# The end of an FFT-convolution kernel on one core: the last scan slot split by frequency, the last transposes by token, the stores cut smaller, the residual added per channel quarter

## The chip, the cores and the metric

The kernel runs on one core of a Trainium2 chip (trn2). It is one program. The metric is the device time of one execution in microseconds (us), as the median of several runs. The profile is of one execution by itself and has its own time. The engines are called as the profile calls them: PE (matmuls), DVE (vector), ACT (scalar), POOL (GpSimd) and SP, which only issues DMA transfers; "SPq" and "ACTq" are DMA issues on SP's and ACT's queue.

## The reference

The input `u` has 2048 tokens (L) of 512 channels (D). Its layer norm feeds two branches, which are multiplied and added to the input:

```python
x = A_u
xn = _layernorm(x)
s = irfft(rfft(xn, 2L) * rfft(K, 2L))[:L] + xn * Dskip   # K: a 2048-tap filter per channel, from 128 complex modes
h = gelu_tanh(xn @ w1 + b1)                              # 512 -> 1792
g = silu(h @ w2 + b2)                                    # 1792 -> 512
out = x + s * g
```

Everything is float32.

## The kernel before, in words

The long first part (some 400 us) does the layer norm, both matrix products of the second branch and the filters. A written-out list of tokens fixes its order, and the change does not touch it. The second part does the convolution, and the order there is the order of the code: each engine works through its instructions as `slot` and the lines behind the loop issue them.

The convolution is a two-step Fourier transform with length 2048 = 32 x 64. The channels go in four blocks `b` = 0 to 3 of 128 channels, and every block takes eight slots `g` = 0 to 7. A slot handles four of the 32 outer frequencies:

- `second_dft` (L881): PE makes the inner transform of signal and filter for these frequencies, in a tile `s`, in two PSUM banks.
- `spectrum` (L889): ACT copies the signal half to SBUF (`uh`). `product` (L898): DVE multiplies it with the filter half, in two instructions of 512 elements for each partition, to `t`.
- `combine` (L906, L908): DVE makes real and imaginary part `Y` of the complex product; both its inputs lie in SBUF. It is called once for two slots, in the last block's last two slots once each.
- `back_dft` (L919): PE transforms eight frequencies back into two banks `sa`, one for each `a`; `es` chooses which of its four steps `e` run.
- `back_out` (L929): `sa` goes to SBUF (`Z`). `turn` (L935): DVE transposes 32x32 blocks of `Z` to `T`, in halves `i` of 1024 elements. `Z` and `T` are kept for each half `h` of the frequencies.
- `last_dft` (L966): PE ends the transform in banks `y`, adding `h` = 0 and `h` = 1. `last_gate` (L973; L979 for the last block): DVE multiplies `y` with the gate `g` read back from memory. `last_add` (L983): adds `x`, by default on POOL. `store` (L988): four DMA transfers, one for each channel group `c`.

The outputs of block `b` are finished in slots 4 to 7 of block `b + 1`. For block 3 nothing follows, so the lines L1098 to L1114 finish it alone: the second half of the last `back_dft`, the `y` products, copies shared by ACT and DVE, transposes, and then two halves of the tokens (0 to 7, 8 to 15 of 16 for each partition), each gated by DVE, added by DVE (5 tokens) and POOL (3 tokens), and stored by four transfers of 128 KB, two on SP's queue and two on ACT's.

A tile is one object for the bookkeeping of waits: where two engines touch the same PSUM bank, one waits for the other. A transfer signals its landing on one of eight semaphores (`DMAHW0` to `DMAHW7` in the order below), in turn, and a transfer whose semaphore was used before waits, on its queue, for the landing of that earlier transfer.

Of the kernel before, what the change touches and what calls it, by code (L numbers as in the profile page):

```python
# [11 lines left out]
F32 = mybir.dt.float32  # L12
# [8 lines left out]
P = 128  # L21
L, D, NS, F = 2048, 512, 128, 1792
G = D // P
NF = F // P
KD = D // P
N1, N2 = 32, 64
NB = 4
# [5 lines left out]
NQ = L // P  # L33
# [135 lines left out]
def kernel(  # L169
# [126 lines left out]
    SB = {}  # L296
# [499 lines left out]
    side, xf, fp = {}, {}, {}  # L796
# [75 lines left out]
    def second_dft(b, g):  # L872
        mc = SB["mc"]
        p = SB["ps"].tile([P, 2, 2, 2, 2, N2], F32, tag="ri", name=f"s2_{b}_{g}", bufs=2)
        for jj in range(2):
            for o in range(2):
                for c in range(2):
                    for ka in range(2):
                        for r in range(2):
                            k, h = 8 * (g // 2) + 4 * ka + 2 * (g % 2) + jj, slice(r * 64, (r + 1) * 64)  # L880
                            PE.matmul(p[ka * 64:(ka + 1) * 64, r, o, :, jj], mc[h, k, ((0, 2), (1, 0))[c][o], :],  # L881
                                      xf[b][h, c, :, k, :], start=(c == 0), stop=(c == 1), skip_group_check=True)
        sp[b, g] = p
# [10 lines left out]
    def product(b, g):  # L894
        p, uh = sp.pop((b, g))
        for i in range(2):
            t = sm[b, g // 2][i].rearrange("p o r (h a) x -> p h o r (a x)", h=2)[:, g % 2]
            V.tensor_mul(t, p[:, i, :, 1].unsqueeze(1).to_broadcast([P, 2, 2, P]), uh)  # L898

    def combine(b, j, c, eng, js=slice(0, 4)):  # L900
        t, w = sm[b, j]
        if (b, j) not in yy:
            yy[b, j] = SB["pm"].tile([P, 2, 4, P], F32, tag="Y", name=f"Y_{b}_{j}", bufs=2)
        Y = yy[b, j][:, c].rearrange("p j (r x) -> p r j x", r=2)
        if c == 0:
            eng.tensor_sub(Y[:, :, js], t[:, 0, :, js], w[:, 1, :, js])  # L906
        else:
            eng.tensor_add(Y[:, :, js], t[:, 1, :, js], w[:, 0, :, js])  # L908
# [13 lines left out]
    def back_out(b, j, eng=A, m=slice(0, N2)):  # L922
        if (b, "Z", j // 2) not in yy:
            yy[b, "Z", j // 2] = SB["pm"].tile([P, N2, 2, N1 // 2], F32, tag="Z", name=f"Z{b}_{j // 2}", bufs=2)
        for a, p in enumerate(yy[b, j, "p"]):
            k = 8 * (j % 2) + 4 * a
            dst = yy[b, "Z", j // 2][:, m, :, k:k + 4]
            src = p.rearrange("p k (c n) -> p n c k", c=2)[:, m]
            A.copy(dst, src) if eng is A else eng.tensor_copy(dst, src)  # L929

    def turn(b, h, i, n=2):
        if i == 0:
# [34 lines left out]
                              start=(h == 0), stop=(h == 1), skip_group_check=True)  # L967

    def last_gate(b):
        g = gx[b][0].rearrange("p n (a c r) -> p r a n c", a=2, r=2)  # L970
        for q in range(G):
            d = g[:, q // 2, q % 2]
            V.tensor_mul(d, gx[b, "y"][q].rearrange("p (n c) -> p n c", c=N1), d)  # L973

    def last_gate_wide(b, n):
        g = gx[b][0].rearrange("p n (a c r) -> p r a n c", a=2, r=2)
# [1 line left out]
            d = g[:, r, :, n]  # L978
            V.tensor_mul(d, gx[b, "w"][r].rearrange("p a (n c) -> p a n c", c=N1)[:, :, n], d)  # L979

    def last_add(b, n, eng=GP):
        g, x = gx[b]
        eng.tensor_add(x[:, n], g[:, n], x[:, n])  # L983

    def store(b, n=slice(0, NQ), qs=(SY,) * G):
        x = gx[b][1]
# [5 lines left out]
    def slot(b, g):  # L992
# [6 lines left out]
        second_dft(b, g)  # L999
        for x in back:  # L1000
            back_dft(*x)
        if u:
# [2 lines left out]
            last_dft(b - 1)  # L1005
        if last and g == 7:
            back_dft(b, 3, (0, 1))
        spectrum(b, g)
        for x in back:
            back_out(*x)  # L1010
        if u:
            first_out(b + 1, *u, engs, A)
        product(b, g)
        if u:
            first_out(b + 1, *u, engs, V)
        if (b, g) == (0, 0):
            new_gate(0)
        if last and g > 5:
            for c in range(2):
                combine(b, i, c, V, slice(2 * g - 12, 2 * g - 10))  # L1020
        elif g % 2:
# [46 lines left out]
    with tc.manual_schedule():  # L1068
# [43 lines left out]
        last_add(b, slice(8, 13), V)  # L1112
        last_add(b, slice(13, NQ), GP)
        store(b, hi, (SY, A, SY, A))  # L1114
    pz.close()
    p2.close()

# [27 lines left out]
```

## Time and profile before

| what | us |
|---|---|
| median of three runs | 553.2 (553.17 to 555.86) |
| the profiled execution, its time | 554.85 |
| the profiled execution, its span from first to last instruction | 553.1 |
| busy: PE, DVE, ACT, POOL | 526.9, 456.0, 387.0, 289.8 |

The time of an execution is 1.75 us longer than its span (554.85 against 553.1); the rest lies outside the instructions. In the rows, times are from the span's start; "x2" means two instructions merged in one row, and the text in brackets gives the engine's idle time before the row and what ended it. The granted clock was 0.994 over the span.

### The profile page before, as it was taken

Reading aid. Unit: us, or ns where it says so; the run is one execution under the profiler, and the core shown is the slowest. Engines: PE = TensorE matmul, PEld = TensorE weight load, DVE = VectorE, ACT = ScalarE, POOL = GpSimd, SP = SyncE. Lnnn points to the kernel's source line nnn. Section 1 sums busy time; section 2 is a strip of 40 time slices with the busy share of each in tenths; the row PEclk is TensorE's granted clock in tenths of the full one; section 3 lists DMA queues with packets and bytes.
Section 4 is the critical chain, followed back from the end, with each engine's and each line's share of the span. In section 5 each row is a group of like instructions: output and inputs, shape, how many; then the busy total and the mean of one; then the engine's idle time right before and its main releaser. Section 6 shows DMA issues by size and latency. Waiting matters only on the chain.

```text
span 553.1 us, 17527 instructions
## 1 busy us (share of the span) xinstructions
PE 526.9 (95%) x7439; PEld 419.6 (76%) x7439; DVE 456.0 (82%) x684; ACT 387.0 (70%) x566; POOL 289.8 (52%) x385
## 2 busy tenths in 40 slices
PE   8899999999999999999999999999999999999971
PEld 7577777777777777777777777777878997989860
DVE  5899998999998899997987978968247667688784
ACT  3589997986698998768989798997264553534320
POOL 5639586685967669957809846641220203413042
PEclk9999999999999999999999999999999999999997
DMA  8959336266659293446068129403896485536943
GB/s 186 291 161 317 86 96 204 69 190 208 178 173 278 101 290 104 140 113 179 24 194 241 46 72 203 79 20 108 314 372 92 112 153 106 164 81 159 208 99 76
DMA packets 110538, 86.92 MB, mean 157 GB/s; under 512 B 43414, under 2 KB 88730, under 8 KB 110460
## 3 DMA queue, kind: packets, MB, share of 16 engines
q1 hardware_dynamic: 100592, 67.45, 46.3%
q0 software_dynamic: 8768, 17.83, 10.7%
q8 instruction: 58, 0.95, 0.7%
q10 hardware_dynamic: 1100, 0.53, 0.4%
q14 instruction: 20, 0.16, 0.1%
HBM read 52.23 MB, written 33.55 MB: 155 GB/s over the span
## 4 chain that ended last, share of the span: by engine, by line
PE 71%; DVE 19%; issue 5%; POOL 2%; DMA 1%; ACT 1%; POOLq 0%; SPq 0%; DVEq 0%; ACTq 0%
PE s L881 10%; PE z L290 8%; PE z L291 7%; PE z L292 7%; PE f L251 7%; PE f L253 7%; PE f L252 7%; PE s L861 6%; PE kg L651 5%; PE sa L919 4%; PE ph L590 2%; DVE hl L277 2%; DVE e L636 2%; PE y L966 1%; DVE e L640 1%
## 5 line engine op out<-in xcount | busy, mean ns | idle before, releaser
L613 POOL TENSOR_TENSOR mm<-mm,rc 128x32 f32<-128x32 f32 (+4 forms) x150 | 111.4, 742 | 11.8
L290 PE MATMUL z<-w2h,hh 128*128 128x512 f32 x224 | 97.9, 437 | 0.0
L251 PE MATMUL f<-xh,w1h 128*128 128x512 f32 x220 | 91.9, 418 | 0.1
L292 PE MATMUL z<-w2h,hl 128*128 128x512 f32 x224 | 88.6, 395 | 1.0 <-DVE hl L277 1.0
L291 PE MATMUL z<-w2l,hh 128*128 128x512 f32 x224 | 88.6, 396 | 0.0
L253 PE MATMUL f<-xh,w1l 128*128 128x512 f32 x220 | 87.0, 395 | 1.5 <-DVE w1l L236 1.5
L252 PE MATMUL f<-xl,w1h 128*128 128x512 f32 x220 | 86.7, 394 | 0.0
L881 PE MATMUL s<-X,mc 64*64 64x128 f32 x2048 | 64.1, 272 | 2.6 <-issue 2.0
L898 DVE TENSOR_TENSOR t<-s,uh 128x512 f32<-128x512 f32 x64 | 41.0, 682 | 30.3 <-ACT uh L889 30.0
L881 PEld LDWEIGHTS s<-X,mc 64*64 64x64 f32 x2048 | 56.0, 133 | 9.4 <-issue 5.6
L292 PEld LDWEIGHTS z<-w2h,hl 128*128 128x128 f32 x224 | 42.1, 188 | 11.8 <-DVE hl L277 1.8
L610 POOL COPY mm<-rc 128x32 f32<-128x32 f32 x30 | 15.7, 524 | 66.4 <-DVE e L643 50.9
L636 DVE TENSOR_TENSOR e<-mm,ra 128x1024 f32<-128x1024 f32 x32 | 46.7, 1459 | 4.6 <-POOL mm L613 3.0
L253 PEld LDWEIGHTS f<-xh,w1l 128*128 128x128 f32 x220 | 41.3, 188 | 12.0 <-DVE w1l L236 2.2
L277 DVE TENSOR_TENSOR hl<-hf,hh 128x512 fp32r<-128x512 f32 x56 | 47.2, 846 | 3.3 <-ACT hh L271 3.3
L290 PEld LDWEIGHTS z<-w2h,hh 128*128 128x128 f32 x224 | 42.5, 190 | 9.0
L604 DVE SCALAR_TENSOR_TENSOR ra<-ra,ph 128x512 f32<-128x512 f32 x64 | 43.6, 682 | 6.8 <-ACT ra L598 5.9
L251 PEld LDWEIGHTS f<-xh,w1h 128*128 128x128 f32 x220 | 41.5, 189 | 9.7 <-ACT hf L265 0.6
L291 PEld LDWEIGHTS z<-w2l,hh 128*128 128x128 f32 x224 | 42.3, 189 | 7.9
L252 PEld LDWEIGHTS f<-xl,w1h 128*128 128x128 f32 x220 | 41.4, 188 | 9.0
L983 POOL TENSOR_TENSOR xb<-gb,xb 128x512 f32<-128x512 f32 x12 | 17.6, 1497 | 53.8 <-DVE gb L973 30.4
L640 DVE TENSOR_TENSOR e<-mm,ra 128x1024 f32<-128x1024 f32 x32 | 45.4, 1420 | 0.0
(171 smaller groups left out, 1104.5 us busy)
## 6 DMA issues: line engine op xcount, KB each, us to landing
x<-in_A_u_dram SPq DMA_DIRECT2D x16, 256.0 KB
xs<-x SPq DMA_DIRECT2D x16, 256.0 KB
xt_h<-xh POOLq DMA_DIRECT2D x4, 1024.0 KB, 5.3
xt_l<-xl POOLq DMA_DIRECT2D x4, 1024.0 KB, 7.8
kgd<-ko SPq DMA_DIRECT2D x32, 128.0 KB
za<-zo SPq DMA_DIRECT2D x4, 1024.0 KB
xh<-xt_h POOLq DMA_DIRECT2D x4, 1024.0 KB, 6.7
xl<-xt_l POOLq DMA_DIRECT2D x4, 1024.0 KB, 10.0
```

What stands on the lines that cost most here:

```text
L251: PE.matmul(p, wh[:, k, :], xh[:, k, :], start=(k == 0), stop=False)
L252: PE.matmul(p, wh[:, k, :], xl[:, k, :], start=False, stop=False)
L253: PE.matmul(p, wl[:, k, :], xh[:, k, :], start=False, stop=(k == KD - 1))
L277: V.tensor_sub(hl, hf, hh)
L290: PE.matmul(z, hh[:, s], wh, start=(f0 == 0 and not rows), stop=False)
L291: PE.matmul(z, hh[:, s], wl, start=False, stop=False)
L292: PE.matmul(z, hl[:, s], wh, start=False, stop=(f0 == FA - 1))
L604: V.scalar_tensor_tensor(ra[:, 0, c], ra[:, 1, c], MAGIC, p, op0=ALU.subtract, op1=ALU.subtract)
L613: GP.tensor_mul(mv[:, :, 0:3:2, w:2 * w], mv[:, :, 0:3:2, 0:w], rc[:, 2 + 2 * i:4 + 2 * i, :].rearrange("p j c -> p c j").unsqueeze(3).to_ ...
L636: V.tensor_mul(e1, m1.unsqueeze(1).to_broadcast([P, 2, CH, N1]), ra[:, :, :, :N1])
L640: V.tensor_mul(e2[:, :, :, :H], m2[:, :, :H].unsqueeze(1).to_broadcast([P, 2, CH, H]), ra[:, :, :, dn])
L881: PE.matmul(p[ka * 64:(ka + 1) * 64, r, o, :, jj], mc[h, k, ((0, 2), (1, 0))[c][o], :], xf[b][h, c, :, k, :], start=(c == 0), stop=(c == 1 ...
```

## The change

- In slot 7 of the last block, `last_second`, `last_product` replace `second_dft`, `spectrum`, `product`: the tile's layout puts the pair of frequencies `jj` outside, and copy, products and `combine` run for each `jj` by itself.
- `last_out` replaces `back_out` for the second half of the last block's frequencies. `Z` is laid out by token half `i` first, and ACT does all the copies, of the steps 0 and 1 of the last `back_dft` before the steps 2 and 3. `last_turn` transposes one token half, and `last_half` makes `y` for that half from all frequencies, with 256 columns instead of 512.
- The second transposition of the first frequency half moves from slot 5 to the end of slot 7.
- The last gates, adds and stores go over the tokens 0-3, 4-7, 8-11, 12-13, 14-15. DVE does all the adds; there are 20 transfers instead of 8.
- For the blocks 0 to 2, POOL adds `x` for each channel quarter `q` right behind that quarter's gate (rows of 32 elements, every second one in memory), and no longer by groups of four tokens. The stores stand where they stood.

```diff
+    def last_second(b, g):
...
+        p = SB["ps"].tile([P, 2, 2, 2, 2, N2], F32, tag="ri", name=f"s2_{b}_{g}", bufs=2)
+        for jj in range(2):
...
+                            PE.matmul(p[ka * 64:(ka + 1) * 64, r, jj, o], mc[h, k, ((0, 2), (1, 0))[c][o], :],
+                                      xf[b][h, c, :, k, :], start=(c == 0), stop=(c == 1), skip_group_check=True)
+    def last_product(b, g, jj):
+        p, uh = sp[b, g]
+        q = p[:, :, jj].rearrange("p r o u x -> p o r u x")
+        A.copy(uh[:, jj], q[:, :, :, 0])
+        for i in range(2):
+            V.tensor_mul(sm[b, g // 2][i][:, :, :, 2 * (g % 2) + jj],
+                         q[:, i, :, 1].unsqueeze(1).to_broadcast([P, 2, 2, N2]), uh[:, jj])
+        for c in range(2):
+            combine(b, g // 2, c, V, slice(2 * (g % 2) + jj, 2 * (g % 2) + jj + 1))
+    def last_out(b, j, k0, k1):
...
+        for i in range(2):
+            for a, p in enumerate(yy[b, j, "p"]):
+                k = 8 * (j % 2) + 4 * a
+                A.copy(yy[b, "Z", 1][:, i, :, :, :, k + k0:k + k1],
+                       p[:, k0:k1].rearrange("p k (c g i m) -> p i g m c k", c=2, g=4, i=2)[:, i])
+    def last_turn(b, i):
...
+        V.transpose(yy[b, "T", 1][:, i].rearrange("p g m c -> p (g m c)"),
+                    yy[b, "Z", 1][:, i].rearrange("p g m c k -> p (g m c k)"))
+    def last_half(b, i):
+        for g in range(G):
+            for q in range(G):
+                r = slice(q * N1, (q + 1) * N1)
+                PE.matmul(gx[b, "y"][q][g * N1:(g + 1) * N1, i * 256:(i + 1) * 256], SB["gc"][r, 1],
+                          yy[b, "T", 1][r, i, g].rearrange("p m c -> p (m c)"),
+                          start=False, stop=True, skip_group_check=True)
     def last_gate(b):
-        g = gx[b][0].rearrange("p n (a c r) -> p r a n c", a=2, r=2)
+        g, x = (t.rearrange("p n (a c r) -> p r a n c", a=2, r=2) for t in gx[b])
         for q in range(G):
-            d = g[:, q // 2, q % 2]
+            d, e = g[:, q // 2, q % 2], x[:, q // 2, q % 2]
             V.tensor_mul(d, gx[b, "y"][q].rearrange("p (n c) -> p n c", c=N1), d)
+            GP.tensor_add(e, d, e)
...
-        if g == (5 if last else 6):
+        if last and g in (5, 7):
+            turn(b, 0, (g - 5) // 2)
+        if not last and g == 6:
             turn(b, 0, 0)
             turn(b, 0, 1)
...
-        if b and g in (4, 5, 6, 7):
-            last_add(b - 1, slice(4 * g - 16, 4 * g - 12))
-            if g in (5, 7):
-                store(b - 1, slice(4 * g - 20, 4 * g - 12))
+        if b and g in (5, 7):
+            store(b - 1, slice(4 * g - 20, 4 * g - 12))
...
         b = NB - 1
+        last_out(b, 3, 0, 2)
         back_dft(b, 3, (2, 3))
         last_dft(b, (0,), wide=True)
-        for i, eng in enumerate((A, V)):
-            back_out(b, 3, eng, slice(32 * i, 32 * i + 32))
+        last_out(b, 3, 2, 4)
         for i in range(2):
-            turn(b, 1, i)
-            last_dft(b, (1,), range(2 * i, 2 * i + 2))
-        lo, hi = slice(0, 8), slice(8, NQ)
-        last_gate_wide(b, lo)
-        last_add(b, slice(0, 5), V)
-        last_add(b, slice(5, 8), GP)
-        store(b, lo, (SY, A, SY, A))
-        last_gate_wide(b, hi)
...
+            last_turn(b, i)
+            last_half(b, i)
+        for n in (slice(0, 4), slice(4, 8), slice(8, 12), slice(12, 14), slice(14, NQ)):
+            last_gate_wide(b, n)
+            last_add(b, n)
+            store(b, n, (SY, A, SY, A))
```

The first place is the end of slot 7 and what follows, on DVE. The names are output`<-`inputs; `t_3_6` are the two product tiles, `Y_3` the combined spectrum, `Z_1`, `T_1` the second frequency half, `T_0` the first. Before:

```order
L898 TENSOR_TENSOR t_3_6_7524<-s_3_7_7535,uh_7_7578 128x4x128 [waits Activation_49]
L898 TENSOR_TENSOR t_3_6_7525<-s_3_7_7535,uh_7_7578 128x4x128
L906 TENSOR_TENSOR Y_3_7531<-t_3_6_7524,t_3_6_7525 128x2x2x64 [waits DVE_49]
L908 TENSOR_TENSOR Y_3_7531<-t_3_6_7524,t_3_6_7525 128x2x2x64
L929 COPY Z_1_7526<-sa_3_0_7568 128x64x4 [waits DMASW5_49,Activation_49]
L929 COPY Z_1_7526<-sa_3_1_7569 128x64x4 [waits Activation_49]
L935 STREAM_TRANSPOSE T_1_7619<-Z_1_7526 128x1024
```

Now (DVE):

```order
L918 TENSOR_TENSOR t_3_6_7525<-s_3_7_7537,uh_7_7570 128x4x64 [waits Activation_49]
L918 TENSOR_TENSOR t_3_6_7526<-s_3_7_7537,uh_7_7570 128x4x64
L929 TENSOR_TENSOR Y_3_7534<-t_3_6_7525,t_3_6_7526 128x128 [waits DVE_49]
L931 TENSOR_TENSOR Y_3_7534<-t_3_6_7525,t_3_6_7526 128x128
L918 TENSOR_TENSOR t_3_6_7525<-s_3_7_7537,uh_7_7570 128x4x64 [waits Activation_49]
L918 TENSOR_TENSOR t_3_6_7526<-s_3_7_7537,uh_7_7570 128x4x64
L929 TENSOR_TENSOR Y_3_7534<-t_3_6_7525,t_3_6_7526 128x128 [waits DVE_49]
L931 TENSOR_TENSOR Y_3_7534<-t_3_6_7525,t_3_6_7526 128x128
L981 STREAM_TRANSPOSE T_0_7466<-Z_0_7307 128x1024
L966 STREAM_TRANSPOSE T_1_7630<-Z_1_7527 128x1024 [waits Activation_49] x2
```

Four instructions became eight of half the size, DVE's two copies of `Z_1` are gone, and a transposition of `T_0` stands in their place. On ACT, the same place, now (before, it had one copy of `uh_7` with 512 elements and two of `Z_1` with 64x4):

```order
L916 COPY uh_7_7570<-s_3_7_7537 128x256 [waits DVE_49,PE_49,Activation_49]
L916 COPY uh_7_7570<-s_3_7_7537 128x256 [waits DVE_49]
L960 COPY Z_1_7527<-sa_3_0_7571 128x64x2 [waits PE_49]
L960 COPY Z_1_7527<-sa_3_1_7572 128x64x2 [waits PE_49]
L960 COPY Z_1_7527<-sa_3_0_7571 128x64x2
L960 COPY Z_1_7527<-sa_3_1_7572 128x64x2
L960 COPY Z_1_7527<-sa_3_0_7571 128x64x2 [waits PE_49]
L960 COPY Z_1_7527<-sa_3_1_7572 128x64x2 [waits PE_49]
```

The second `uh_7` copy waits for DVE: for the products of the first pair, which read the same PSUM tile. The first one waits for the last matmul of the slot, not for the last one of its pair.

The second place is POOL's adds for block 2 in the last block's slots (`xb` holds `x` and then the result, `gb` the gated product). Before:

```order
L983 TENSOR_TENSOR xb_7113<-gb_6937,xb_7113 128x512 [waits DMAHW3_49,DMAHW4_49,DMAHW2_49,DMAHW5_49,DMAHW1_49,DMAHW6_49,DMAHW0_49,DMAHW7_49,DVE_49,Pool_49]
L983 TENSOR_TENSOR xb_7113<-gb_6937,xb_7113 128x512
L983 TENSOR_TENSOR xb_7113<-gb_6937,xb_7113 128x512 [waits DMAHW6_49,DMAHW7_49,DMAHW1_49,DMAHW0_49]
L983 TENSOR_TENSOR last<-last 128x384 [waits DMAHW3_49,DMAHW4_49,DMAHW2_49,DMAHW5_49,DVE_49,Activation_49]
L983 TENSOR_TENSOR last<-last 128x384 [waits DMAHW6_49,DMAHW1_49,DMAHW7_49,DMAHW0_49,DVE_49]
```

Now (POOL, with block 1's adds ahead):

```order
L1020 TENSOR_TENSOR xb_6519<-gb_6294,xb_6519 128x16x32 [waits DMAHW4_49,DMAHW3_49,DMAHW5_49,DMAHW2_49,DMAHW6_49,DMAHW1_49,DMAHW7_49,DMAHW0_49,DVE_49]
L1020 TENSOR_TENSOR xb_6519<-gb_6294,xb_6519 128x16x32 [waits DVE_49] x3
L1020 TENSOR_TENSOR xb_7113<-gb_6939,xb_7113 128x16x32 [waits DMAHW3_49,DMAHW4_49,DMAHW2_49,DMAHW5_49,DMAHW1_49,DMAHW6_49,DMAHW0_49,DMAHW7_49,DVE_49,Pool_49]
L1020 TENSOR_TENSOR xb_7113<-gb_6939,xb_7113 128x16x32 [waits DVE_49] x3
L1189 UNCONDITIONAL_BRANCH
```

There are four adds for a block as before, but the first waits for the first of DVE's four gates and not for the last, and POOL has nothing left to do for the last block. The third place is SP's queue at the end, now (before, four transfers 32x8x128; ACT's queue has the same ten):

```order
L1035 DMA out_dram<-last 32x4x128 [waits DMAHW3_49,DVE_49]
L1035 DMA out_dram<-last 32x4x128 [waits DMAHW4_49]
L1035 DMA out_dram<-last 32x4x128 [waits DMAHW6_49,DVE_49]
L1035 DMA out_dram<-last 32x4x128 [waits DMAHW0_49]
L1035 DMA out_dram<-last 32x4x128 [waits DMAHW2_49,DVE_49]
L1035 DMA out_dram<-last 32x4x128 [waits DMAHW4_49]
L1035 DMA out_dram<-last 32x2x128 [waits DMAHW6_49,DVE_49]
L1035 DMA out_dram<-last 32x2x128 [waits DMAHW0_49]
L1035 DMA out_dram<-last 32x2x128 [waits DMAHW2_49,DVE_49]
L1035 DMA out_dram<-last 32x2x128 [waits DMAHW4_49]
```

Each of the five token pieces has two rows here; `DMAHW2`, `DMAHW4` come a second time in the fifth piece and `DMAHW4` in the third after the first. With eight semaphores for twenty transfers, the third piece's transfers wait for the landing of the first's, the fourth's for the second's, and the fifth's for the third's.

More of the change, by code (lines that the diff above doesn't have):

```diff
@@ L929, in back_out @@
             A.copy(dst, src) if eng is A else eng.tensor_copy(dst, src)
+    def last_out(b, j, k0, k1):
+        if (b, "Z", 1) not in yy:
+            yy[b, "Z", 1] = SB["pm"].tile([P, 2, 4, 8, 2, N1 // 2], F32, tag="Z", name=f"Z{b}_1", bufs=2)
+        for i in range(2):
[4 more added lines that the diff above has]
+    def last_turn(b, i):
+        if i == 0:
+            yy[b, "T", 1] = SB["pm"].tile([P, 2, 4, 8, N1], F32, tag="T", name=f"T{b}_1", bufs=2)
+        V.transpose(yy[b, "T", 1][:, i].rearrange("p g m c -> p (g m c)"),
[7 more added lines that the diff above has]
+                          start=False, stop=True, skip_group_check=True)
     def turn(b, h, i, n=2):
@@ L998, in slot @@
         engs = (A, A, A, V) if g in (2, 3) else (A, A, A, A)
-        second_dft(b, g)
+        (last_second if last and g == 7 else second_dft)(b, g)
         for x in back:
@@ L1007, in slot @@
             back_dft(b, 3, (0, 1))
[L1008 to L1015, printed above, removed]
+            for jj in range(2):
+                last_product(b, g, jj)
+        else:
+            spectrum(b, g)
+            for x in back:
+                if x == (NB - 1, 2):
+                    last_out(*x, 0, 4)
+                else:
+                    back_out(*x)
+            if u:
+                first_out(b + 1, *u, engs, A)
+            product(b, g)
+            if u:
+                first_out(b + 1, *u, engs, V)
         if (b, g) == (0, 0):
             new_gate(0)
-        if last and g > 5:
+        if last and g == 6:
             for c in range(2):
-                combine(b, i, c, V, slice(2 * g - 12, 2 * g - 10))
-        elif g % 2:
+                combine(b, i, c, V, slice(0, 2))
+        elif g % 2 and not (last and g == 7):
             for c in range(2):
```

14 lines of the change are left out of this document (9 added, 5 removed).

## The prediction, made before the changed kernel ran

> **What bounds the kernel now.** I read the page's head first, then the last rows of the chain of waits, then the timeline of the last 30 us, since the chain gives up there.
>
> ```profile
> span 553.1 us, 17527 instructions
> PE 71%; DVE 19%; issue 5%; POOL 2%; DMA 1%; ACT 1%; POOLq 0%; SPq 0%; DVEq 0%; ACTq 0%
> 495.53 3.77 PE sa L919 x64
> 499.30 1.91 PE s L881 x64
> 527.97 3.35 POOL xb L983 x2
> 531.32 12.56 issue
> 545.86 1.67 POOLq L1141
> ```
>
> PE carries the chain through the slots (rows at 495 and 499). The chain's 12.56 us of "issue" before the end has no releaser, so that stretch has to be read by hand:
>
> ```profile
> 522.84 2.49 DVE L973 TENSOR_TENSOR gb<-y,gb 128x512 f32<-128x512 f32 x4
> 525.43 1.29 DVE L898 TENSOR_TENSOR t<-s,uh 128x512 f32<-128x512 f32 x2
> 525.46 5.85 POOL L983 TENSOR_TENSOR xb<-gb,xb 128x512 f32<-128x512 f32 x4 [23.36 <-DMA last<-in_A_u_dram]
> 526.76 1.75 DVE L906 TENSOR_TENSOR Y<-t,t 128x512 f32<-128x512 f32 x1
> 528.44 1.75 DVE L908 TENSOR_TENSOR Y<-t,t 128x512 f32<-128x512 f32 x1
> 530.24 1.83 PE L919 MATMUL sa<-tcn,Y 64*128 64x128 f32 x28 [1.09 <-DVE Y L908]
> 532.00 1.98 PE L881 MATMUL s<-X,mc 64*64 64x128 f32 x64
> 534.09 0.59 ACT L889 COPY uh<-s 128x512 f32<-128x512 f32 x1 [0.91 <-ACT Z L929]
> 534.71 1.29 DVE L898 TENSOR_TENSOR t<-s,uh 128x512 f32<-128x512 f32 x2 [0.27 <-ACT uh L889]
> 536.03 0.42 DVE L906 TENSOR_TENSOR Y<-t,t 128x256 f32<-128x256 f32 x1
> 536.37 0.42 DVE L908 TENSOR_TENSOR Y<-t,t 128x256 f32<-128x256 f32 x1
> 536.51 1.27 PE L919 MATMUL sa<-tcn,Y 64*128 64x128 f32 x16 [1.08 <-DVE Y L906]
> 537.82 0.65 ACT L929 COPY Z<-sa 128x256 f32<-128x256 f32 x2 [3.14 <-PE sa L919]
> 538.22 0.76 DVE L929 COPY Z<-sa 128x256 f32<-128x256 f32 x2 [1.43 <-ACT Z L929]
> 538.89 2.36 DVE L935 STREAM_TRANSPOSE T<-Z 128x1024 f32<-128x1024 f32 x2
> 541.31 1.09 PE L966 MATMUL y<-T,gc 32*32 32x512 f32 x16
> 542.47 1.29 DVE L979 TENSOR_TENSOR last<-y,last 128x512 f32<-128x512 f32 x2 [1.22 <-PE y L966]
> 543.79 0.83 DVE L983 TENSOR_TENSOR last<-last 128x640 f32<-128x640 f32 x1
> 543.89 1.59 POOL L983 TENSOR_TENSOR last<-last 128x384 f32<-128x384 f32 x1 [12.58 <-issue]
> 545.51 3.12 SPq L988 DMA_DIRECT2D out_dram<-last  x4
> 545.90 1.63 POOL L983 TENSOR_TENSOR last<-last 128x384 f32<-128x384 f32 x1 [0.41 <-DVE last L979]
> ```
>
> This is one relay: combine to 530.19, PE to 533.98, ACT, DVE, PE to 537.78, copies, transposes, PE to 542.40, gate, add, store. No engine is full; each waits for the one before. The last POOL add ends at 547.53, and the span ends 5.6 us later:
>
> ```profile
> DMA  0000049999999889999997689999999999753100
> 546.25:551.25 5.00, 0.00 (x0) 0.00 (x0) 0.43 (x1) 0.00 (x0) 1.28 (x1) 0.50 0.93 207
> SPq L1141 <- DMA out_dram<-last: 2.8, 1, 2.8
> ```
>
> The first row is the DMA engines' load from 545.5 to 551.8 in 40 slices of 0.16 us: the first data moves at 546.3, 0.8 us after the first issue, and the last at 551.4; in between (second row) they are 93% busy at 207 GB/s. So from 546.3 the megabyte of block 3 is limited by the transfers: 1.05 MB / 207 GB/s = 5.1 us. SP waits 2.8 us behind its last issue (545.51 + 3.12 = 548.6), so to about 551.5; closing takes another 1.6.
>
> **The change, step by step** (places in us of this trace).
>
> *1. POOL's adds of block 2 start earlier.* Alone, an add takes 1.27. The two combines at 526.76 took 1.75 each beside them; 128x256 takes 0.42 and 128x640 0.83, so 128x512 should take 0.69. The products at 525.43, with one input in PSUM, took 1.29 beside POOL as at 534.71 without it. So a combine and an add exclude each other: a combine waits for the running add and then takes its turn. Now the first add starts behind the first gate, 523.5 + 0.15, and the next follow every 1.23: 524.9, 526.1, ending at 527.35. The first combine then runs to 527.9, the fourth add to 529.1, the second combine to 529.65 instead of 530.19: -0.5. What is unknown is an add on every second element:
>
> ```profile
> 525.46 1.27 POOL L983 TENSOR_TENSOR xb<-gb,xb 128x512 f32<-128x512 f32 x1 [23.36 <-DMA last<-in_A_u_dram]
> L834 POOL COPY in<-raw 128x1024 f32<-128x1024 f32 x6 | 11.9, 2014 | 26.5 <-PE s L861 23.5 <-issue 3.0
> ```
>
> The lower bound is 1.27. The upper is the copy, whose input steps by 32 elements: 1.97 ns an element, for two inputs of 512 that is 2.01. With 2.01 the adds end at 525.7, 527.7, 530.2 and the second combine at 530.75: +0.55. I take 1.27, since a step of two is nearer to a step of one than of 32. The Trainium skill (GPSIMD Engine Reference, "Performance pitfalls for Q7 kernels") puts the extra cost, about half, at a step of more than 8 bytes; here it is 8 bytes, so by it 1.27 holds, and past it 1.9 would move the sum as the upper bound does.
>
> In blocks 1 and 2 the same move is hidden by PE, which runs through there (rows at 495, 499); without that cover it would be another 0.5 each. SP's four stores of slot 5 wait for the fourth add, about 1.2 later than for the second; behind them stand loads needed a slot or more later, so: nothing.
>
> *2. Slot 7 in halves.* ACT's copies by size:
>
> ```profile
> L929 ACT COPY Z<-sa 128x256 f32<-128x256 f32 x2 | 0.6, 376 | 3.1 <-PE sa L919 3.1
> L929 ACT COPY Z<-sa 128x512 f32<-128x512 f32 x2 | 1.1, 589 | 2.8 <-PE sa L919 2.8
> ```
>
> PE's share starts 0.5 earlier and ends at 533.45. The first `uh` copy waits for all of it (534.0 at its end: ACT takes 0.38 for 256), products 0.43 + 0.34 to 534.75, combine (two of 128: 0.29 each by the line through 0.42 and 0.83, 0.21 apart) to 535.3. The second `uh` copy waits for the first products: 534.85 to 535.25; products to 536.05, combine to 536.6. Before: 536.79. So the halves eat 0.3 of the 0.5. ACT's four new copies of the steps 0 and 1 (128 elements; by the line through the two rows 0.27 each, 0.16 apart) run from 535.3 to 536.05, and PE's step 2, which writes the same banks, waits for them; step 2 to 536.7, step 3 to 537.35, against 537.78. Bounds for this step alone: -0.3 if the waits overlap, +0.6 if ACT's narrow copies cost like wide ones.
>
> *3. Copies.* Before, DVE's copies started behind ACT's (538.22) and the transposes at 538.89, 1.1 after PE. Two copies of 128 elements take 0.43: the first transpose can start at 537.85, 0.5 after PE: another -0.6. Bounds: 0 (copies writing two elements at a time run at half speed) and -0.7. The moved transpose of `T_0` (half of 2.36) lies at 536.5 to 537.75 on DVE, just covered; without cover up to +0.5. In slot 5 its place becomes free, where PE is waited for.
>
> *4. Transposes and last `y`.* Two transposes as before: to 540.2. Matmuls by width:
>
> ```profile
> L966 PE MATMUL y<-T,gc x64: 587/598/612, 537.7 to 541.8; 32*32 32x512 f32 x64
> L881 PE MATMUL s<-X,mc 64*64 64x128 f32 x64 | 2.0, 272 | 0.0
> ```
>
> `last_half` has 16 matmuls of 256 columns on 16 tiles of the array where 8 of 512 took 1.09. Two passes of 256 columns less, at 0.85 ns a column by these rows: -0.4, with a few ns for each added start. Bounds: 0 and -0.5. First gate at 541.0, against 542.47.
>
> *5. Gates, adds, stores.* A piece of four tokens: gates 0.35 + 0.4, add 0.69, together 1.36 from piece to piece; of two tokens 0.85. No POOL, which took 1.59 for three tokens beside DVE. Pieces are ready at 542.5, 543.9, 545.3, 546.2, 547.05; the first store goes 3.0 earlier than at 545.51, the last piece is ready 0.5 earlier than POOL's end at 547.53. The stores' issues (ns, shortest, median, longest; starts):
>
> ```profile
> L988 SPq DMA_DIRECT2D out_dram<-last x4: 315/384/722, 545.5 to 547.9; - x4
> ```
>
> Each queue issues two stores for a piece, 0.4 each. Semaphores: the third piece waits for the first's landing. Data of the first moves from 543.3, 256 KB take 1.25, so it has landed by about 545.2 (0.6 for the rest): no wait. The fourth, for the second: hardly. The fifth, ready at 547.05, waits for the third: issued 545.35 to 545.75, its data ends at 543.3 + 0.75 MB / 207 = 547.2, landed 547.3 to 548.0. So the last issue is at 548.0, its data ends at 549.0, landed 549.4, end of span 551.0. Before: data 551.4, landed 551.5, end 553.1. Bounds of this step: the last piece without any wait, -0.6; every landing as late as the last one now (issue at 547.9, landed at 551.5: 3.6), +1.8 in all (first rival). I take the middle way because the queue is shorter than before while the first pieces move.
>
> The Trainium skill (DMA: Bandwidth & Descriptors, "Rules for kernel authors") speaks against this step: transfers should be coalesced, and under 64 KB one pays mostly overhead; the last eight here have 32 KB. Its fixed 2.0 us for a transfer ("Anatomy of one DMA") would have the three waves land by 542.5 + 3 x 2.15 = 549.0, no later than above; the 3.6 from the rows shows that here it can be more.
>
> **Sum:** span 553.1 - 2.1 = 551.0: steps 1 and 2 -0.4, 3 -0.6, 4 -0.4, 5 -0.7. The profiled execution's own time, 554.85, would become 552.75. It stands 1.65 over the median of the runs; against the median, 553.2 - 2.1 = 551.1.
>
> **Rivals.**
>
> *A. The semaphores pace the stores (slower).* At the fifth piece. If each landing takes the 3.6 of the last one now, the waves land at 546.1, 549.7, 553.3, and the span ends at 554.9: +1.8, time 555.0. The point of decision is 542.5 + 3 x L = 551.5, a landing of 3.0. For it: 3.6 was measured. Against: that one stood behind 1 MB at 93% load, and here 0.25 MB come at a time.
>
> *B. POOL's strided adds are slow.* Step 1 gives +0.55 in place of -0.5, the rest stays: 552.2.
>
> *C. The halves don't run as halves.* The second `uh` waits for the first products, step 2 for ACT, and if small copies cost like wide ones steps 2 to 4 bring nothing: -0.5 of step 1 and -0.7 of step 5 remain: 552.0.
>
> *D. No wait in step 5.* The landings come early; the last store issues at 547.5 and all ends 0.6 earlier; with both good bounds of 3 and 4: 550.2.
>
> **From this to the numbers.** Chances: the forecast 0.47, A 0.08, B 0.12, C 0.15, D 0.18. The forecast with its own range of +-0.6, B and C lie within 550.4 to 552.8. To leave out no more than 0.2 I take in D and the near part of A, which gives 549.9 to 553.1. A measurement of this kernel tells about 0.5%, 2.8 us, from no change: faster means below 550.4, which is D's better half and the forecast's lower edge, 0.2; slower means above 556.0, A with a further delay, 0.03; the same, 0.77.
>
> **What would show it.** Step 1: POOL's adds starting near 523.7, combines of about 1.15 and 1.8, the second ending near 529.65. Step 2: second `uh` copy behind the products, last matmul of `sa` near 537.4. Step 3: no gap of 1.1 before the transposes. Step 4: 16 matmuls of 256 columns within 0.7. Step 5: DVE without gaps over the five pieces, first issue near 542.5; and a wait of SP or ACT for a landing ahead of the last issues: about 0.9, where A has over 2. A strided add over 1.3, or landings over 3 us, would make the prediction wrong.

## The result, and the profile after

The changed kernel took 553.06 us (median of 20 runs, 551.93 to 555.57) against 554.79 (20 runs, 553.17 to 557.73) for the kernel before on the same chip. The ratio is 0.9971 with a 95% interval of [0.9958, 0.9983], so 0.9 to 2.3 us were gained, 1.6 in the middle. The three runs that the prediction's base stood on (553.2) lay 1.6 below the median of twenty. The ratio of each run below is against runs of the kernel before on that run's own chip.

The head of the page after, the shares of its chain of waits, and the last two of the 55 longest pieces of that chain:

```profile
span 552.2 us, 17612 instructions
PE 74%; DVE 17%; issue 3%; DMA 3%; ACT 1%; SPq 0%; DVEq 0%; ACTq 0%
527.52 1.91 DVE Y L929
529.43 1.91 DVE Y L931
```

Where the chain of before passed through POOL's adds (527.97), this one passes through the two combines that wait for them; from there it goes on in short pieces to DVE's last add at 548.04. The timeline of the end follows (start, duration, engine and line, tiles, shapes, and in brackets the idle time ahead and its releaser):

```profile
523.61 2.48 DVE L1019 TENSOR_TENSOR gb<-y,gb 128x512 f32<-128x512 f32 x4
524.43 6.35 POOL L1020 TENSOR_TENSOR xb<-gb,xb 128x512 f32<-128x512 f32 x4 [22.91 <-DVE gb L1019]
526.20 1.29 DVE L898 TENSOR_TENSOR t<-s,uh 128x512 f32<-128x512 f32 x2
527.52 1.91 DVE L929 TENSOR_TENSOR Y<-t,t 128x512 f32<-128x512 f32 x1
529.36 1.98 DVE L931 TENSOR_TENSOR Y<-t,t 128x512 f32<-128x512 f32 x1
531.39 1.83 PE L942 MATMUL sa<-tcn,Y 64*128 64x128 f32 x28 [1.32 <-DVE Y L931]
533.15 1.98 PE L909 MATMUL s<-X,mc 64*64 64x128 f32 x64
535.24 0.37 ACT L916 COPY uh<-s 128x256 f32<-128x256 f32 x1 [0.79 <-ACT Z L960]
536.43 0.37 ACT L916 COPY uh<-s 128x256 f32<-128x256 f32 x1 [0.82 <-DVE t L918]
537.37 1.33 PE L942 MATMUL sa<-tcn,Y 64*128 64x128 f32 x16 [1.15 <-ACT Z L960]
538.72 0.78 ACT L960 COPY Z<-sa 128x128 f32<-128x128 f32 x4 [1.23 <-PE sa L942]
539.20 2.36 DVE L966 STREAM_TRANSPOSE T<-Z 128x1024 f32<-128x1024 f32 x2
541.61 0.73 PE L973 MATMUL y<-T,gc 32*32 32x256 f32 x32 [0.40 <-DVE T L966]
542.48 0.76 DVE L1026 TENSOR_TENSOR last<-y,last 128x256 f32<-128x256 f32 x2 [0.92 <-PE y L973]
543.99 5.77 SPq L1035 DMA_DIRECT2D out_dram<-last  x10
548.04 0.42 DVE L1030 TENSOR_TENSOR last<-last 128x256 f32<-128x256 f32 x1
```

The first row stood at 522.84 before. So 0.77 us of this execution were lost ahead of the place where the end begins. This kernel and four of those below that are the same up to that row had it at 522.39 to 524.87: between single executions that place moves by more than the change is worth, and whether the new adds of the blocks 0 and 1 cost anything ahead of it is not shown. All comparisons therefore use distances from this row, called G2 (first gate of block 2), from the end of PE's last `s` (S7), and from the first gate of block 3 (G3). Landings are read from the trace's landing records.

| us | G2 to second combine's end | G2 to S7 | S7 to G3 | G3 to last landing | landing to end | G2 to end |
|---|---|---|---|---|---|---|
| before | 7.34 | 11.14 | 8.49 | 9.32 | 1.28 | 30.23 |
| after | 7.73 | 11.52 | 7.36 | 8.64 | 1.03 | 28.55 |
| difference | +0.39 | +0.38 | -1.13 | -0.68 | -0.25 | -1.68 |

The 1.68 agree with the 1.6 of the timed runs. Everything behind S7 came as forecast or a little better; ahead of it 0.4 were lost where 0.5 were to be gained. The durations of POOL's four adds of block 2 (ns: shortest, median, longest), first before, then after, show why:

```profile
L983 POOL TENSOR_TENSOR xb<-gb,xb x4: 1270/1490/1722, 525.5 to 529.6; 128x512 f32<-128x512 f32 x4
L1020 POOL TENSOR_TENSOR xb<-gb,xb x4: 1518/1520/1944, 524.4 to 528.8; 128x512 f32<-128x512 f32 x4
```

An add that never waits takes 1.27 in the contiguous form (the shortest of before) and 1.52 on every second element. The long ones of both rows lie beside a combine and hold a wait for it.

SP's waits in the changed kernel from 539 us on (us in all, how often, longest):

```profile
SPq L1035 <- DMA out_dram<-last: 0.4, 1, 0.4
SPq L1189 <- DMA out_dram<-last: 0.8, 4, 0.3
```

The first is the wait of a store for an earlier landing, 0.4. It lies between 547.7 and 548.5, ahead of the fourth piece: that piece was ready 5.12 behind G3, and the second piece's store, whose semaphore it uses again, landed at 5.46. The second stands behind the last issue, where before had 2.8 in one piece. The DMA engines' load in the 10 us from G3, 40 slices of 0.25 us, before and then after:

```profile
DMA  0000000000000003999998999779999998520000
DMA  0000000005999939979949999975756660000000
```

Before, the data start 3.75 behind G3 and end at 9.0, nearly without a gap. After, they start at 2.25 and end at 8.25, and the last seven slices run at 50 to 70%, with the small stores of the last two pieces. The issues (ns: shortest, median, longest) suggest why:

```profile
L1035 SPq DMA_DIRECT2D out_dram<-last x10: 315/408/458, 544.0 to 549.3; - x10
```

At the median of 0.41 us an issue, two queues hand out no more than 2 x 32 KB / 0.41 us = 160 GB/s. This is an estimate from these rows; the seven slices moved 138 GB/s in the mean, where before had 207 over the whole transfer. No run tests it by itself.

### The profile page after: what moved, and what is told of

Read it like the earlier page. It is cut to its first block, busy times and chain, and to the rows that moved or that the text cites. A ratio compares the mean times of both kernels' runs of the same rounds, so it can differ in the third digit from the quotient of the medians.

```text
span 552.2 us, 17612 instructions
## 1 busy us (share of the span) xinstructions
PE 526.0 (95%) x7471; PEld 418.9 (76%) x7471; DVE 456.2 (83%) x695; ACT 388.1 (70%) x575; POOL 288.5 (52%) x383
## 4 chain that ended last, share of the span: by engine, by line
PE 74%; DVE 17%; issue 3%; DMA 3%; ACT 1%; SPq 0%; DVEq 0%; ACTq 0%
PE s L881 10%; PE z L290 8%; PE z L291 7%; PE z L292 7%; PE f L251 7%; PE f L253 7%; PE f L252 7%; PE s L861 6%; PE kg L651 5%; PE sa L942 5%; DMA w2s<-in_B_w_dram 2%; PE ph L590 2%; DVE e L636 2%; DVE hl L277 2%; PE y L1012 1%
## 5 line engine op out<-in xcount | busy, mean ns | idle before, releaser
L881 PE MATMUL s<-X,mc 64*64 64x128 f32 x1984 | 62.4, 272 | 3.7 <-issue 3.1
L898 DVE TENSOR_TENSOR t<-s,uh 128x512 f32<-128x512 f32 x62 | 39.7, 682 | 31.5 <-ACT uh L889 31.3
L881 PEld LDWEIGHTS s<-X,mc 64*64 64x64 f32 x1984 | 54.3, 133 | 10.7 <-issue 7.1
L265 ACT ACTIVATE hf<-f,b1s 128x512 f32<-128x512 f32 x56 | 38.5, 690 | 9.3 <-PE f L253 4.7
```

## The experiments

The theory after the result: (a) the loss ahead of S7 is the strided add, 0.25 longer than taken, four times in a row ahead of the second combine, and nothing else; (b) steps 2 to 4 and 5 each give what the distances show. Rivals: the loss comes from the adds' early start itself; the gain behind S7 comes from another part than the one named; the small stores cost as much as they bring.

**The adds alone, on the kernel before** (per channel quarter in `last_gate`; those by tokens taken out).

```diff
+            GP.tensor_add(e, d, e)
...
-            last_add(b - 1, slice(4 * g - 16, 4 * g - 12))
```

> The kernel before with this one part alone: POOL adds x per channel quarter right behind each gate. Theory: second combine 7.73 us behind the start of block 2's first gate (before: 7.35), end of span 30.6 (before: 30.23): slower by 0.4. Rival (early start wins, as was predicted): 6.8 and 29.7.

```profile
524.71 2.48 DVE L973 TENSOR_TENSOR gb<-y,gb 128x512 f32<-128x512 f32 x4
525.53 6.35 POOL L974 TENSOR_TENSOR xb<-gb,xb 128x512 f32<-128x512 f32 x4 [22.92 <-DMA last<-gd]
530.46 1.97 DVE L908 TENSOR_TENSOR Y<-t,t 128x512 f32<-128x512 f32 x1
```

G2 to the second combine's end was 7.73, G2 to the end 30.78 (of the 0.55 over before, 0.18 lie between G3 and the last landing). Timed: 555.49 us, ratio 1.002 [0.9996, 1.0044]. The distance is the changed kernel's to 0.01, so the adds alone cost 0.39 there; the time agrees (+1.1, -0.2 to +2.4) without proving it.

**The change with the adds of before** (that `last_add` line back, the quarter adds gone).

> The changed kernel with one part undone: in blocks 0 to 2 POOL adds x as before, by groups of four tokens behind the fourth gate. Measured from the start of block 2's first gate in the last block (before: second combine ends 7.35 us later, span ends 30.23 later; changed kernel: 7.73 and 28.59). Theory (an add on every second element takes 1.52 instead of 1.27, and all four come ahead of the second combine, since DVE's combine and POOL's add exclude each other): 7.35 and 28.2, so 0.4 faster than the changed kernel. Rival (the combine is not what the end waits for): 28.6, no change.

Its rows that answer to those above, in the timeline:

```profile
523.41 2.48 DVE L1019 TENSOR_TENSOR gb<-y,gb 128x512 f32<-128x512 f32 x4
526.03 5.85 POOL L1029 TENSOR_TENSOR xb<-gb,xb 128x512 f32<-128x512 f32 x4 [23.38 <-DVE gb L1019]
529.00 1.75 DVE L931 TENSOR_TENSOR Y<-t,t 128x512 f32<-128x512 f32 x1
541.90 0.76 DVE L1025 TENSOR_TENSOR last<-y,last 128x256 f32<-128x256 f32 x2 [0.92 <-PE y L973]
```

The adds start 2.62 behind G2 in place of 0.82 and take 0.5 less in all; three of them come ahead of the second combine in place of four and it ends at 7.34, as in the kernel before; G2 to the end is 28.13, 0.42 under the changed kernel. Timed 552.21, ratio 0.9957 [0.994, 0.9975]; the times alone do not tell it from the changed kernel. So the added part of the change that was to gain 0.5 lost 0.4, from both sides.

**What an add costs by its step.** The adds all behind the fourth gate, with another form in each block:

```diff
+        for q in (3, 0, 1, 2):
+            cs = slice(32 * q, 32 * q + 32) if b == 0 else slice(q, P, 4)
+            d, e = (t[:, :, cs] for t in gx[b]) if b < 2 else (g[:, q // 2, q % 2], x[:, q // 2, q % 2])
+            GP.tensor_add(e, d, e)
```

> The kernel with the strided adds behind the fourth gate, with another form of the adds in the blocks 0 and 1: block 0 adds rows of 32 neighbouring channels (step one, 16 rows), block 1 every fourth channel (step 16 bytes), block 2 every second as before. It measures the disputed cost by itself. If the step of two costs (every second access lost): block 0 at 1.27 us, block 2 at 1.52, block 1 at or above 1.52. If the short rows cost (16 rows of 32 in place of one run): all three 1.52. If the step matters only above 8 bytes: 1.27 or 1.52 in blocks 0 and 2 alike, and about 1.9 in block 1.

POOL's adds in the blocks 0, 1 and 2 (ns: shortest, median, longest):

```profile
L1023 POOL TENSOR_TENSOR xb<-gb,xb x4: 1258/1492/1721, 461.7 to 465.9; 128x512 f32<-128x512 f32 x4
L1023 POOL TENSOR_TENSOR xb<-gb,xb x4: 2157/2396/2605, 495.0 to 502.2; 128x512 f32<-128x512 f32 x4
L1023 POOL TENSOR_TENSOR xb<-gb,xb x4: 1518/1779/1949, 525.7 to 530.9; 128x512 f32<-128x512 f32 x4
```

The shortest are the ones without a wait: 1.26 for rows of 32 neighbours, 1.52 for every second element, 2.16 for every fourth. The rows cost nothing, the step costs. (One execution, 551.13 us, so no verdict on time.)

**The strided adds, all behind the fourth gate.** Same durations, later start (the loop begins with the fourth gate's quarter, so every add waits for that gate):

```diff
+            d = g[:, q // 2, q % 2]
+            V.tensor_mul(d, gx[b, "y"][q].rearrange("p (n c) -> p n c", c=N1), d)
+        for q in (3, 0, 1, 2):
             d, e = g[:, q // 2, q % 2], x[:, q // 2, q % 2]
-            V.tensor_mul(d, gx[b, "y"][q].rearrange("p (n c) -> p n c", c=N1), d)
             GP.tensor_add(e, d, e)
```

> The changed kernel with the same four strided adds, but all of them behind the fourth gate. Theory (what counts is how many adds get their turn ahead of each combine): one add ahead of the first combine and one more ahead of the second, which ends 2.62 + 1.47 + 0.55 + 1.42 + 0.55 = 6.6 us behind the start of the first gate (changed kernel: 7.73), end of span 27.5: 1.1 faster than the changed kernel. Rival (slow strided adds cost, wherever they start; an earlier start can only help): 7.8 or more, and 28.7 or more.

```profile
524.89 2.48 DVE L1019 TENSOR_TENSOR gb<-y,gb 128x512 f32<-128x512 f32 x4
527.50 6.80 POOL L1022 TENSOR_TENSOR xb<-gb,xb 128x512 f32<-128x512 f32 x4 [22.48 <-DMA last<-gd]
529.48 1.99 DVE L931 TENSOR_TENSOR Y<-t,t 128x512 f32<-128x512 f32 x1
```

The adds start 1.8 later than in the changed kernel, two of them come ahead of the second combine, and it ends at 6.58, 1.15 earlier. G2 to the end is 27.45; timed 551.66, ratio 0.9941 [0.9917, 0.9966]. That is 0.76 earlier than with the contiguous adds of before (7.34), of which three come ahead: here the number of adds ahead of the combine counts for more than the duration of one. It hangs on little: the first combine begins 3.9 behind G2; a contiguous first add is over by then and the second just begun (3.85), a strided first add still runs (to 4.12).

**Contiguous adds, held out of the combines' way.** POOL first copies one element per partition of the combine's result, and so waits for it:

```diff
+        if b and g == 4:
+            last_add(b - 1, slice(0, 4))
+        if b and (g == 5 or last and g == 6):
+            hold = SB["pm"].tile([P, 1], F32, tag="hold", name=f"hold{b}_{g}", bufs=2)
+            GP.tensor_copy(hold, yy[b, i][:, 1, 1 if g == 6 else 3, 127:128])
+        if b and g == 5:
+            for k in (1, 2):
+                last_add(b - 1, slice(4 * k, 4 * k + 4))
...
```

(the fourth add behind slot 6's combine)

> The changed kernel with contiguous adds by four tokens, held away from the combines: one behind the fourth gate, two behind slot 5's combine, one behind slot 6's (in the last block; three behind slot 5's in the others), held by a one-element POOL copy that reads the combine's result. Theory: both combines run in 0.7, the second ends 5.2 us behind the start of the first gate, PE goes on without a wait at 5.8 instead of 7.8; end of span 26.7, so 1.9 faster than the changed kernel and 3.5 faster than before (0.65%). Rival (the exclusion only moves to slot 6's combine, or PE waits for something else there): no more than 1.0 faster than the changed kernel, end at 27.6.

```profile
523.05 2.48 DVE L1019 TENSOR_TENSOR gb<-y,gb 128x512 f32<-128x512 f32 x4
527.01 0.69 DVE L929 TENSOR_TENSOR Y<-t,t 128x512 f32<-128x512 f32 x1
527.62 0.68 DVE L931 TENSOR_TENSOR Y<-t,t 128x512 f32<-128x512 f32 x1
```

Without an add beside them the combines take 0.69 and 0.68 where the changed kernel shows 1.91 and 1.98; the second one ends at 5.26. G2 to the end fell to 27.24 only, 0.5 short of the expectation: G3 to the last landing was 9.15 against 8.64. Timed 551.71, ratio 0.9958 [0.9939, 0.9976]. The trace shows four landings that came 0.2 apart behind all the others, from 548.70 to 549.26; a kernel below with the same adds and four pieces does not have them.

**The last slot in one piece** (`second_dft`, `spectrum`, `product`, `combine` for the last slot as before, the rest as changed).

> The changed kernel with the last slot's transform, copy, products and combine in one piece; the copies, transposes, adds and stores as changed. It undoes the first half of step 2 alone. The prediction's reading (the halves cost 0.3, since the second copy waits for the first products and PE's step 2 for ACT's copies): from the end of the slot's transform to the first gate 7.05 us against 7.35 in the changed kernel, time 0.3 lower. The reading of the changed kernel's trace (3.57 from the transform to the last matmul of sa in halves, 3.80 in one piece): 7.6, time 0.2 higher. A change over 0.5 either way speaks against both.

```profile
532.23 1.98 PE L881 MATMUL s<-X,mc 64*64 64x128 f32 x64
538.52 2.37 DVE L966 STREAM_TRANSPOSE T<-Z 128x1024 f32<-128x1024 f32 x2 [0.34 <-ACT Z L960]
541.81 0.76 DVE L1026 TENSOR_TENSOR last<-y,last 128x256 f32<-128x256 f32 x2 [0.92 <-PE y L973]
```

From S7 (534.21) to G3 it takes 7.60: the halves gain 0.24, where the prediction had them cost. In this execution they do not reach the end: the last landing came 8.45 behind G3 and not 8.64, with no wait of SP for a landing, so G2 to the end was 28.60 against 28.55. Why the landings differ is taken up with the four pieces. Timed 552.85, ratio 0.9971 [0.9954, 0.9988], not told apart from the changed kernel.

**The last copies shared with DVE** (`last_out` gives the second token half to DVE, as before).

> The changed kernel with the last copies of sa shared as in the kernel before: ACT copies the first token half, DVE the second; all else as changed. It undoes step 3 alone. Theory (DVE's copies come behind ACT's and ahead of the transposes, as before): transposes 0.9 to 1.0 after the last matmul of sa against 0.5, from the end of the slot's transform to the first gate 7.8 to 7.9 us against 7.36. Rival (a shared second half costs nothing, since DVE copies while ACT does): 7.36 to 7.5.

```profile
538.64 1.33 PE L942 MATMUL sa<-tcn,Y 64*128 64x128 f32 x16 [1.15 <-ACT Z L963]
539.99 0.44 ACT L963 COPY Z<-sa 128x128 f32<-128x128 f32 x2 [1.23 <-PE sa L942]
540.47 0.45 DVE L965 COPY Z<-sa 128x128 f32<-128x128 f32 x2
540.85 2.35 DVE L970 STREAM_TRANSPOSE T<-Z 128x1024 f32<-128x1024 f32 x2
```

DVE's copies stand behind ACT's and ahead of the transposes, which start 0.88 behind PE in place of 0.50; S7 to G3 took 7.72. So it is the theory's order, at 0.36 of the expected 0.44 to 0.54: taking DVE out of the copies brings 0.36 to 0.38 of step 3's 0.6. One execution (555.56 us, span 553.8) gives no verdict on time, and its G2 lay 1.3 later than the changed kernel's.

**The end as before: two halves, eight stores.**

> The changed kernel with the end of the kernel before (two token halves, POOL sharing the adds, eight stores); all else as changed. It undoes step 5 alone. Theory (the first store's early start is worth about 0.7): from the last block's first gate to the last landing 9.3 us as before, against 8.66 in the changed kernel; from block 2's first gate to the end of the span 29.3 against 28.6; time 0.7 above the changed kernel's. Rival (twenty small stores pay for themselves in overhead and in waits for landings, and the megabyte takes as long either way): 8.7 and 28.6, the same time as the changed kernel.

G3 to the last landing was 9.34, as the theory had it, and G2 to the end 29.50, 0.2 over the theory's 29.3. Timed 553.87, ratio 0.9986 [0.9969, 1.0003]; the intervals of this and of the changed kernel overlap, so the 0.95 rests on the traces. The Trainium skill's advice to coalesce (DMA: Bandwidth & Descriptors, "Rules for kernel authors") did not hold for this cut: stores of 128 KB cut to 64 and 32 KB ended 0.70 earlier, and the first of them left 1.5 earlier (1.51 behind G3 against 3.04). The run puts POOL's share of the adds back too, so what the cutting brings without that is not shown.

**Four pieces in place of five, with held adds, and then in the changed kernel alone.**

```diff
-        for n in (slice(0, 4), slice(4, 8), slice(8, 12), slice(12, 14), slice(14, NQ)):
+        for n in (slice(0, 4), slice(4, 8), slice(8, 12), slice(12, NQ)):
```

> The kernel with contiguous adds held behind the combines, with four store pieces of four tokens (16 stores) in place of five (20). The fifth piece's stores, and their wait for the third piece's landing, are gone; DVE ends 0.4 earlier (four pieces every 1.39 against 5.98), but the last store is twice as large. Theory (the last piece's transfer and landing set the end, and its size costs more than the wait): gate to last landing 8.6 to 8.9, the same as or 0.2 above five pieces. Rival (the wait of 0.4 for a landing is what the fifth piece costs): 8.2, time 0.4 below five pieces, 551.3.

G3 to the last landing was 8.18, landing to end 1.27, G2 to the end 26.50, and the time 550.75, ratio 0.9931 [0.9918, 0.9945], the lowest time of this study, though the late strided adds' interval overlaps its own. The expectation that the larger last store would eat the gain fell. But the held adds were in it too, so:

> The changed kernel with four store pieces of four tokens (16 stores) in place of five (20), nothing else. Held adds with four pieces showed 8.18 from the first gate to the last landing, held adds with five 9.15, the changed kernel 8.64. Theory (the fifth piece and its wait for a landing cost 0.45): 8.2 to 8.3 here too; the closing after the last landing 0.25 longer (1.28 with eight and with sixteen stores, 1.03 with twenty), so the end 0.2 earlier than in the changed kernel, time 552.9. Rival (the 8.18 came from the earlier adds and stores of block 2, which here come as in the changed kernel): 8.6 or more, and the end 0.2 later.

8.18 again, then 1.28, and 28.32 to the end, 0.23 under the changed kernel, as the theory had it. Timed 552.06, ratio 0.9955 [0.9936, 0.9974]. Among SP's waits for this end only the waits for DVE are left ahead of the stores:

```profile
SPq L1035 <- DVE last L1030: 10.0, 4, 8.4
SPq L1189 <- DMA out_dram<-last: 1.5, 2, 1.4
```

So the change from five pieces to four brought 0.46 at the landing, and the 8.18 does not come from the held adds. DVE's end lies 0.3 earlier with four pieces, so the 0.46 is not the wait for a landing alone.

Not all of it comes from the pieces. The DMA view of the changed kernel's 10 us from G3 has this row:

```profile
q14 instruction: 1, 0.01, 0.4%
```

It is one packet of 8 KB on the queue `instruction`, between the stores. In the changed kernel and in four traces above (the adds of before, both kinds of adds behind the fourth gate, the shared copies) it starts 3.8 to 3.9 behind G3; there the first store of the second piece lands at 5.4 to 5.5 and the last store at 8.61 to 8.70. With the last slot in one piece and with four even pieces it starts behind the last landing, and the second piece's first store lands at 4.6. With held adds and five pieces it starts at 7.14, and there the last four landings straggle to 9.15. Where the packet lies outside the stores, five pieces end at 8.45 and four at 8.18: a fifth piece then costs 0.27. No run moves the packet alone, and late landings occur without it (9.32 before, 8.68 in the next run), so that it delays the landings is argued and not shown.

**Four uneven pieces, with held adds** (5, 5, 4 and 2 tokens).

> The kernel with contiguous adds held behind the combines and four store pieces, now of 5, 5, 4 and 2 tokens in place of 4, 4, 4 and 4. DVE's work is the same; the first store goes 0.25 later, the last store is half as large. Theory (behind the last piece there is no wait for a landing, so its size is what is left): data of the pieces end 4.0, 5.65, 6.9 and 7.5 after the first gate at 207 GB/s, the last landing 7.8 to 7.9 against 8.18; time 0.3 lower, 550.4. Rival (the queue of data since the first store sets the end, the sizes only share it out): 8.2 to 8.4, time the same or 0.2 higher.

8.68, worse than either expected. Timed 551.98, ratio 0.9958 [0.994, 0.9975]. The DMA load from G3 in 0.25 us slices, for pieces of 4, 4, 4, 4 and then for 5, 5, 4, 2:

```profile
DMA  0000000005999938999939999579899000000000
DMA  0000000000499899779989979789993000000000
```

The data start a slice later and end at 7.75 as with even pieces; it is the landings that come late, those of four stores mixed up to 8.68, where with even pieces one store after the other landed. So this theory of the last store's size fell. Why the landings trail the data by 0.9 here was not settled.

## Why the prediction was right in part, and which step failed

- *Step 1, POOL's adds* (-0.5, from an add of 1.27): this is the step that failed, by the size of its term and not by its mechanism. The adds started 0.82 behind the gate as forecast, they came ahead of the combines in the order forecast, and a combine and an add excluded each other as forecast. But a strided add takes 1.52: "a step of two is nearer to a step of one than of 32" took the lower bound unchanged, without a row for a step of two. The prediction's own sign of being wrong, a strided add over 1.3, came. Four adds stand ahead of the second combine, one every 1.47 in place of 1.23, so 4 x 0.235 = 0.94 were added and -0.54 became about +0.40; +0.39 was measured (shown by the adds alone, by the change without them, and by the form test). That rival B's +0.55 is near this is luck: with its adds of 2.01 three come ahead of the second combine, where the trace has four of 1.52. No run starts adds at a step of one early, so that these would have gained the 0.54 is not shown. The Trainium skill's limit (GPSIMD Engine Reference, "Performance pitfalls for Q7 kernels"), with no extra cost up to 8 bytes and about half past it, is not what these runs show for this add: 8 bytes cost 20% and 16 bytes 70%.
- What the working of step 1 did not weigh is how many adds stand ahead of the second combine, each with its error of price. Started early, all four adds come ahead of the second combine, in the forecast as in the trace; started where they were, three do; 1.8 later in the strided form, two. The early start had bought 1.8 us of time for one more add ahead, and paid for the length of all four.
- *Step 2* was forecast to eat 0.3 at the second combine and 0.1 at the last matmul of `sa`; the halves gain 0.24 against one piece. From S7 to the last matmul of `sa` it took 3.57, forecast 3.9, before 3.81. The two waits named (second `uh` behind the first products, PE behind ACT's copies) are both in the rows, 0.82 and 1.15; they share 0.2.
- *Step 3* was right: transposes 0.50 behind PE in place of 1.11, so -0.61; the undone half accounts for 0.38, and the rest, by the rows, is that two copies of 128 elements (0.44) end before two of 256 (0.65).
- *Step 4*: transposes' start to first gate 3.28 against 3.58, so -0.30 for -0.4. No run undoes this step alone.
- *Step 5* was right in its size, -0.68 for -0.7: the first store 1.51 behind G3, DVE without gaps to 548.46. SP's wait for a landing was 0.4 and not 0.9, and it came ahead of the fourth piece and not of the fifth. The last issue still came 7.04 behind G3, where the forecast has 7.0; that the size agrees so well is in part luck. Rival A had landings over 3 us; those read here took 1.7 to 2.7 from the issue for 64 KB and 1.6 for 32 KB, and it stayed out. The fixed 2.0 us that the prediction takes from the Trainium skill (DMA: Bandwidth & Descriptors, "Anatomy of one DMA") stands there for transfers issued from GpSimd; these stores went out on SP's and ACT's queues.
- Not foreseen: the closing behind the last landing, 1.03 in place of 1.28 (the prediction's 1.6 counts from SP's last landing at 551.5; ACT's came at 551.79). It is 1.27 to 1.28 with 8 and with 16 stores and 1.02 to 1.04 with 20 in every trace here; the cause stays open.

The sum: -2.1 forecast, -1.68 in the trace: step 1 missed by +0.9, steps 2 to 4 by -0.2, the closing by -0.25. The forecast of 551.1 missed 553.06 mostly by its base (1.6): the profiled execution's own 554.85, which the prediction set aside for the median of three runs, was near the median of twenty (554.79), and 552.75, the forecast from it, lies 0.3 from the result. Two of its figures are 0.1 off by its own terms (rival D comes to 550.3, the lower end with +-0.6 to 550.5); nothing hangs on them. The chance of "within 0.5%" had been put at 0.77, and 0.29% is within it.

## What to carry to other kernels

When POOL and DVE take turns on the same memory, count the instructions that will stand ahead of the one on the critical path, and place POOL's work behind it: holding three adds back brought 2.1 us at that place (7.34 to 5.26), while starting them early, in strided form, cost 0.4. With four pieces at the end, the held adds ended the kernel 1.8 earlier than the early strided ones (28.32 to 26.50). Keep POOL's operands at a step of one, even in short rows. At a kernel's end, start the first store early, and stop cutting where, by the estimate above, the issues no longer keep the DMA engines busy or a store has to wait for the semaphore of an earlier one: here four pieces of 64 KB stores were better than five with 32 KB stores at the end.

## What the runs showed of the hardware

- POOL's add of 128x512 float32: 1.26 us in rows of 32 neighbours, 1.27 in one run, 1.52 at a step of two elements, 2.16 at four.
- A DVE instruction with both inputs in SBUF waits for the whole running POOL add (0.69 became 1.75 to 1.99), one with an input in PSUM does not (1.29 beside POOL as without it). The Trainium skill says so (SBUF — State Buffer, "SBUF: two separate sides": an exclusive lock for the whole instruction), and the traces agree. In the changed kernel the third add started 0.15 us ahead of the first combine, and the combine waited for all of it.
- Two kernels whose last data moved by 7.75 us behind the first gate had their last landing 0.5 us apart (8.18 and 8.68).
